# Block-sparse attention feeding a gMLP: one matmul at a time in the attention's slots, and a changed ending

## The chip, the cores and the metric

One core of a Trainium2 chip runs the whole program. The metric is the device time of one execution in microseconds; the times before are 11 executions with a median of 226.93 us, from 226.41 to 228.16. The engines are named as in the profile: PE (matrix multiplication; its weight loads have a row of their own, PEld), DVE (vector), ACT (activation), POOL (general purpose) and SP (which here only issues transfers).

## The reference, cut to what matters

Four batches, eight heads, 768 positions, 64 channels a head. Attention is masked in blocks of 32 positions (neighbours, first and last block, three sampled blocks a row); its output, with heads side by side, is the input x of a gated MLP that also mixes positions.

```
scores = where(mask, q @ k.T / sqrt(64), -1e9)          # 768 x 768 per head
attn   = softmax(scores)
x      = attn @ v                                        # heads joined: (4, 768, 512)
h      = relu(x @ w_in)                                  # (4, 768, 1024)
u, v   = h[..., :512], h[..., 512:]
v_n    = (v - mean(v)) / sqrt(var(v) + 1e-6)
v_s    = w_spatial @ v_n + b_spatial[:, None]            # mixes the 768 positions
out    = (u * v_s) @ w_out                               # (4, 768, 512)
```

## The kernel before, in words

Operands are bf16, sums are kept in PSUM in fp32. The 32 heads are worked in 16 pairs (`p` 0 to 15, four pairs to a batch). The order of instructions on every engine is the order in which the Python loop writes them down (a manual schedule): no planner moves anything. Each engine works off its own list in order, and a pool of tiles with a tag and a number of buffers (`bufs`) makes an instruction wait until the tile that had the buffer last is done with.

The loop at L461 goes through *slots*, twelve to a pair, six to a head. In a slot:

- `qk_exp` (L284) makes 128 rows of scores for one head: two matmuls of 384 columns into a PSUM tile of tag "sc" (two buffers), and one exp of 768 columns on ACT, which empties it into `a_all`.
- then come pieces of preparation of later pairs in fixed slots: `split_pair` (L275, slots 5 and 9) copies transposed k and q of the next pair on DVE, two copies each; `prepare` (L116, slot 7) casts k, q and v of pair p+2 to bf16 on POOL (`nat_k`, `nat_q`, `vv`); `tr_dma` (slot 10) has SP transpose them.
- then gMLP work of the batch before, if there is any (below).
- `av` (L298), seven slots behind `qk_exp`: six matmuls of 65 columns for one block of 128 queries, into tag "av". After the sixth block of a head, `norm` (L312) divides by the softmax sums on DVE. After each pair, x is transposed (`xtr`, L334): by SP for three pairs of a batch, by PE and a copy on DVE for the fourth.

The gMLP of a batch is 24 *units* (`moe_units`, L360), four groups of six: v (L376) and u (L399) are four matmuls of 512 columns each, s (the spatial product, L421) six, o (L437) four: 108 matmuls. Each unit has a PSUM tile of tag "moe" (two buffers, shared with transposes) and is followed by what empties it: v by relu on DVE (`vsb`), and by statistics of the row (`stats`, `mv`), every third v also by `std` and `rstd` on POOL; u by relu on ACT (`un`), and by the normalised `vn` on DVE; s by the gate on DVE (`gn`) and a transpose by SP (`gt`); o by a copy (`osb`, ACT for even ones and DVE for odd ones) and its transfer to `out` by SP. Below, v0 to v5, u0 to u5, s0 to s5 and o0 to o5 are these units.

The units of a batch become available in slot 8 of the pair after its last, and are handed to the next 48 slots: each slot adds its share of nanoseconds to a budget, and a whole unit is written down where the budget covers half of it:

```
budget += sum(u[0] for u in moe_q) / slots_left
slots_left -= 1
while moe_q and budget >= moe_q[0][0] / 2:
    ns, run = moe_q.popleft()
    run()
    budget -= ns
```

There are only 46 slots left for the third batch; what is not handed out by then comes after the loop (L525), one unit ahead of the last transpose of x, the rest behind it. The fourth batch then runs alone: its units take their PSUM tiles in turn from the tags "moe", "av" and "sc" (`moe_ps`, L352), v's relu is on ACT, and `gn` is transposed by PE (`g_tr`, L412).

Of the kernel before, what the change touches and what calls it, by code (L numbers as in the profile page):

```python
# [11 lines left out]
BF16 = mybir.dt.bfloat16  # L12
I32 = mybir.dt.int32
AF = mybir.ActivationFunctionType
# [12 lines left out]
def kernel(  # L27
# [16 lines left out]
    nc = tc.nc  # L44

    B, H, S, D = q.shape
# [3 lines left out]
    NCH = S // 128  # L50
    HALF = S // 2
    DM = H * D
    DFF = moe_w_in.shape[1]
    DH = DFF // 2
    NDM = DM // 128
    NDH = DH // 128
    NG = H // 2
    NP = B * NG
# [6 lines left out]
    psum = ctx.enter_context(tc.tile_pool(name="psum", bufs=1, space=bass.MemoryType.PSUM))  # L65
# [4 lines left out]
    w_in_t = const.tile([128, NDM, DFF], BF16)  # L70
    w_out_t = const.tile([128, NDH, DM], BF16)
    ws_nat = const.tile([128, NCH, S], BF16)
    w_spt = const.tile([128, NCH, S], BF16)
# [134 lines left out]
    for r in range(NR):  # L208
# [9 lines left out]
                         func=AF.Copy)  # L218
# [13 lines left out]
    tr_ps = {}  # L232
# [89 lines left out]
    def xtr_third(p, third):  # L322
        if third == 0:
            xt_ref[p] = work.tile([128, S], BF16, tag="xt", bufs=8, name="xt")
            tr_ps["x"] = psum.tile([128, S], BF16, tag="moe", bufs=2, name="ps_x")
        ps = tr_ps["x"]
        for c in (2 * third, 2 * third + 1):
            nc.tensor.transpose(out=ps[:, c * 128:(c + 1) * 128], in_=xn_ref[p][:, c],
                                identity=ident)
        if third == 2:  # L330
            xn_ref.pop(p)
            nc.vector.tensor_copy(out=xt_ref[p], in_=ps)
# [14 lines left out]
        nc.sync.dma_start_transpose(out=w_spt[:, :, tcc * 128:(tcc + 1) * 128],  # L347
                                    in_=ws_nat[:, tcc, :])

    tail_tags = deque(["sc", "av", "moe"])  # L350

    def moe_ps(last):  # L352
        if not last:
            return psum.tile([128, 512], FP32, tag="moe", bufs=2, name="ps_moe")
        tail_tags.rotate(1)
        if tail_tags[0] == "sc":
            return psum.tile([128, 1024], FP32, tag="sc", bufs=2, name="ps_sc")[:, 0:512]
        return psum.tile([128, 512], FP32, tag=tail_tags[0], bufs=2, name="ps_t")

    def moe_units(b):  # L360
        last = b == B - 1
        units = []
        un = work.tile([128, NCH, DH], BF16, tag="un", bufs=2)
        vsb = work.tile([128, NCH, DH], BF16, tag="vsb", bufs=2)
        vn = work.tile([128, NCH, DH], BF16, tag="vn", bufs=2)
        gn = work.tile([128, NCH, DH], BF16, tag="gn", bufs=2)
        gt = work.tile([128, NCH, NDH, 128], BF16, tag="gt", bufs=2)
        mv = work.tile([128, NCH, 2], FP32, tag="mv", bufs=2)
        std = work.tile([128, NCH], FP32, tag="std", bufs=2)
        rstd = work.tile([128, NCH], FP32, tag="rstd", bufs=2)  # L370

        def xt(g):
            return xt_ref[b * NG + g]

        for tcc in range(NCH):
            def v_unit(tcc=tcc):  # L376
                ps = moe_ps(last)
                for g in range(NDM):
                    nc.tensor.matmul(out=ps, lhsT=xt(g)[:, tcc * 128:(tcc + 1) * 128],  # L379
                                     rhs=w_in_t[:, g, DH:DFF],  # L380
                                     start=(g == 0), stop=(g == NDM - 1))
                if last:
                    nc.scalar.activation(out=vsb[:, tcc, :], in_=ps, func=AF.Relu)  # L383
                else:
                    nc.vector.tensor_scalar(out=vsb[:, tcc, :], in0=ps, scalar1=0.0,  # L385
                                            scalar2=None, op0=ALU.max)
                stats = work.tile([128, 6], FP32, tag="stats", bufs=2)
                nc.vector.bn_stats(out=stats, in_=vsb[:, tcc, :])  # L388
                nc.vector.bn_aggr(out=mv[:, tcc, :], in_=stats)  # L389
                if tcc % 3 == 2:  # L390
                    cs = slice(tcc - 2, tcc + 1)
                    nc.gpsimd.tensor_scalar(out=std[:, cs], in0=mv[:, cs, 1], scalar1=1e-6,  # L392
                                            scalar2=None, op0=ALU.add)
                    nc.gpsimd.tensor_tensor(out=rstd[:, cs], in0=std[:, cs],
                                            in1=mhalf[:, cs], op=ALU.pow)
            units.append((4 * 215, v_unit))

        for tcc in range(NCH):
            def u_unit(tcc=tcc):  # L399
                ps = moe_ps(last)  # L400
                for g in range(NDM):
                    nc.tensor.matmul(out=ps, lhsT=xt(g)[:, tcc * 128:(tcc + 1) * 128],  # L402
                                     rhs=w_in_t[:, g, 0:DH],
                                     start=(g == 0), stop=(g == NDM - 1))
                nc.scalar.activation(out=un[:, tcc, :], in_=ps, func=AF.Relu)
                nc.vector.tensor_scalar(out=vn[:, tcc, :], in0=vsb[:, tcc, :],
                                        scalar1=mv[:, tcc, 0:1],
                                        scalar2=rstd[:, tcc:tcc + 1],
                                        op0=ALU.subtract, op1=ALU.mult)
            units.append((4 * 215, u_unit))  # L410

        def g_tr(tcc):  # L412
            ps = psum.tile([128, S], BF16, tag="moe", bufs=2, name="ps_g")
            for dhc in range(NDH):
                nc.tensor.transpose(out=ps[:, dhc * 128:(dhc + 1) * 128],
                                    in_=gn[:, tcc, dhc * 128:(dhc + 1) * 128],
                                    identity=ident)
            act_copy(gt[:, tcc].rearrange("p c n -> p (c n)"), ps[:, 0:DH])

        for tcc in range(NCH):  # L420
            def s_unit(tcc=tcc):  # L421
                ps = moe_ps(last)
                for sc in range(NCH):
                    nc.tensor.matmul(out=ps, lhsT=w_spt[:, sc, tcc * 128:(tcc + 1) * 128],  # L424
                                     rhs=vn[:, sc, :],
                                     start=(sc == 0), stop=(sc == NCH - 1))
                nc.vector.scalar_tensor_tensor(out=gn[:, tcc, :], in0=ps,  # L427
                                               scalar=b_col[:, tcc:tcc + 1],
                                               in1=un[:, tcc, :], op0=ALU.add, op1=ALU.mult)
                if not last:  # L430
                    nc.sync.dma_start_transpose(out=gt[:, tcc], in_=gn[:, tcc, :])
                elif tcc > 0:
                    g_tr(tcc - 1)
            units.append((6 * 215, s_unit))

        for tcc in range(NCH):
            def o_unit(tcc=tcc):  # L437
                if last and tcc == 1:
                    g_tr(NCH - 1)
                ps = moe_ps(last)  # L440
                for dhc in range(NDH):
                    nc.tensor.matmul(out=ps, lhsT=gt[:, tcc, dhc, :],  # L442
                                     rhs=w_out_t[:, dhc, :],
                                     start=(dhc == 0), stop=(dhc == NDH - 1))
                osb = work.tile([128, DM], FP32, tag="osb", bufs=6)
                if tcc % 2 == 0:
                    nc.scalar.activation(out=osb, in_=ps, func=AF.Copy)
                else:
                    nc.vector.tensor_copy(out=osb, in_=ps)  # L449
                nc.sync.dma_start(  # L450
                    out=out[b].rearrange("(p c) d -> c p d", c=NCH)[tcc], in_=osb)
            units.append((4 * 215, o_unit))
        return units


    moe_q = deque()
# [4 lines left out]
    for p in range(NP + 1):  # L461
        for s in range(12):
# [38 lines left out]
                if p in (0, 1, 4, 6):  # L501
                    cast_weights((2, 2, 0, 0, 3, 0, 2)[p])
            if moe_q and slots_left > 0:
                budget += sum(u[0] for u in moe_q) / slots_left
                slots_left -= 1
                while moe_q and budget >= moe_q[0][0] / 2:
                    ns, run = moe_q.popleft()
                    run()
                    budget -= ns
            if g >= LAG:  # L510
                ja, qc = divmod(g - LAG, NCH)
                av(ja, qc)
# [6 lines left out]
            if s == 8 and p >= NG:  # L519
                xtr(p - 1)  # L520
                if p % NG == 0:
                    moe_q.extend(moe_units(p // NG - 1))
                    slots_left = 48
                    budget = 0.0
    if moe_q:  # L525
        moe_q.popleft()[1]()
    xtr(NP - 1)
    moe_q.extend(moe_units(B - 1))
    while moe_q:
        moe_q.popleft()[1]()  # L530

# [1 line left out]
_INS = ['q', 'k', 'v', 'sampled_blocks', 'moe_w_in', 'moe_w_spatial', 'moe_b_spatial', 'moe_w_out']  # L533
_OUTS = [((4, 768, 512), 'float32')]
# [25 lines left out]
```

The softmax here doesn't subtract the row's maximum and nothing guards it: scores larger than these inputs give would overflow.

## Time and profile before

| what | value |
|---|---|
| median of 11 runs | 226.93 us (226.41 to 228.16) |
| the profiled execution | 226.58 us, of which the span of its instructions is 224.8 us |
| PE busy | 213.6 us, 95% of the span |
| ACT busy | 171.2 us, 76% |
| DVE busy | 132.2 us, 59% |
| POOL busy | 64.2 us, 29% |
| clock granted to PE | 1.000 throughout |
| pairs 0 to 3, attention alone | up to about 48.8 us |
| batches 0, 1, 2 of the gMLP in the slots | 48.8 to 98.8, 98.8 to 148.9, 148.9 to 195.5 us |
| batch 3 of the gMLP alone | 196.2 to 221.8 us, then the last transfer |

The page of a profile gives busy time by engine, the span in 40 slices, the chain of work that ended last, and groups of instructions with the mean duration of one and what the engine waited for before them. A timeline gives start, duration, engine, line, operation, output and inputs, and how many instructions were merged into the row; a bracket at the end is idle time before the row and who ended it. A matmul's end is modelled, and the next one starts before it: 378 ns are shown for a matmul of 512 columns, but in a row of them one starts every 215 to 216 ns. So PE's real gaps are read from starts: a matmul of 512 columns is taken as 0.2155 us, one of 384 columns as 0.162, one of 65 columns as 0.0325.

### The profile page before, as it was taken

To read this page: it belongs to the slowest core of one execution; us is meant where nothing else is said; L and a number is where in the kernel's file an instruction comes from. 1 tells how busy PE (TensorE), PEld (TensorE's weight loads), DVE (VectorE), ACT (ScalarE), POOL (GpSimd) and SP (SyncE) were. 2 spreads that over 40 slices of the span, in tenths; PEclk is the share of its full clock that TensorE was granted. 3 is DMA by queue.
4 is the path that set the end of the run, shared out by engine and by line. 5 is a ranking of instruction groups with operands and counts; after the bars stand their busy time and mean duration, and the time that the engine had idled before them with its cause. 6 is when DMAs were issued, how large, how long until landed. Compare 5 with 4: busy or idle time off the path is not lost.

```text
span 224.8 us, 5286 instructions
## 1 busy us (share of the span) xinstructions
PE 213.6 (95%) x2119; PEld 130.3 (58%) x2148; DVE 132.2 (59%) x282; ACT 171.2 (76%) x245; POOL 64.2 (29%) x88
## 2 busy tenths in 40 slices
PE   7889999999999999999999999999999999999993
PEld 3557777766656555666556555666565555544551
DVE  6676446359994434379993434469983323674532
ACT  5799999998798677877898668877898666266351
POOL 5336761259483301211273001211230000012000
PEclk9999999999999999999999999999999999999999
DMA  6679989947997994999365665999050424610016
GB/s 178 243 230 389 388 295 394 379 64 97 269 235 145 276 107 135 227 356 297 124 114 204 119 85 169 213 304 242 0 105 3 82 50 83 231 52 0 0 50 235
DMA packets 56093, 40.27 MB, mean 179 GB/s; under 512 B 39300, under 2 KB 51588, under 8 KB 56068
## 3 DMA queue, kind: packets, MB, share of 16 engines
q1 hardware_dynamic: 55780, 39.53, 65.0%
q10 hardware_dynamic: 288, 0.39, 0.6%
q8 instruction: 17, 0.28, 0.5%
q14 instruction: 8, 0.07, 0.1%
HBM read 24.38 MB, written 6.29 MB: 136 GB/s over the span
## 4 chain that ended last, share of the span: by engine, by line
PE 73%; ACT 16%; DMA 5%; issue 2%; SPq 1%; POOL 1%; DVE 1%; POOLq 0%
PE ps L289 20%; ACT a_all L293 16%; PE ps_av L305 11%; PE ps_moe L424 10%; PE ps_moe L379 7%; PE ps_moe L442 7%; PE ps_moe L402 7%; DMA st_k<-in_k_dram 5%; PE ps_t L424 2%; PE ps_t L379 2%; PE ps_t L442 2%; PE ps_t L402 1%; PE ps_sc L424 1%; PE ps_sc L402 1%; PE ps_sc L442 1%
## 5 line engine op out<-in xcount | busy, mean ns | idle before, releaser
L293 ACT ACTIVATE a_all<-ps 128x768 bf16<-128x768 f32 x192 | 143.1, 812 | 30.1 <-PE ps L289 29.9
L289 PE MATMUL ps<-qt,kt 88*128 88x384 bf16 x384 | 93.5, 324 | 4.1 <-ACT a_all L293 2.8
L305 PEld LDWEIGHTS <-a_all 128*128 128x128 bf16 x1152 | 60.3, 98 | 28.5
L305 PE MATMUL ps_av<-vv,a_all 128*128 128x65 bf16 x1152 | 67.6, 194 | 0.0
L289 PEld LDWEIGHTS <-kt 88*128 88x128 bf16 x384 | 28.9, 97 | 8.1 <-issue 5.2
L427 DVE SCALAR_TENSOR_TENSOR gn<-ps_moe,b_col,un 128x512 bf16<-128x512 f32 x18 | 13.5, 751 | 27.2 <-PE ps_moe L424 27.2
L112 POOL CAST vv<-st_v 128x768 bf16<-128x768 f32 x16 | 13.6, 849 | 50.1 <-PE ps_av L305 45.9
L424 PE MATMUL ps_moe<-vn,w_spt 128*128 128x512 bf16 x99 | 24.8, 378 | 0.5
L424 PEld LDWEIGHTS <-w_spt 128*128 128x128 bf16 x144 | 13.8, 97 | 14.3
L392 POOL TENSOR_SCALAR std<-mv 128x3 f32<-128x3 f32 x8 | 1.9, 242 | 65.2 <-DVE mv L389 53.9
L109 POOL CAST nat_k<-st_k 128x768 bf16<-128x768 f32 x15 | 12.5, 833 | 22.0 <-DMA st_k<-in_k_dram 14.6
L319 DVE TENSOR_TENSOR xn<-ps_av,rc 128x384 bf16<-128x384 f32 x32 | 17.8, 557 | 1.1
L442 PE MATMUL ps_moe<-w_out_t,gt 128*128 128x512 bf16 x66 | 18.2, 378 | 0.3
L379 PE MATMUL ps_moe<-w_in_t,xt 128*128 128x512 bf16 x66 | 18.0, 378 | 0.3
L402 PE MATMUL ps_moe<-w_in_t,xt 128*128 128x512 bf16 x66 | 17.7, 378 | 0.3
L388 DVE BATCH_NORM_STATS2 stats<-vsb 128x6 f32<-128x512 bf16 x24 | 16.7, 694 | 1.9 <-ACT vsb L383 1.3
L379 PEld LDWEIGHTS <-xt 128*128 128x128 bf16 x96 | 9.3, 97 | 10.0 <-issue 0.7
L449 DVE COPY osb<-ps_moe 128x512 f32<-128x512 f32 x9 | 6.2, 692 | 15.0 <-PE ps_moe L442 14.9
L402 PEld LDWEIGHTS <-xt 128*128 128x128 bf16 x96 | 9.3, 97 | 9.5
L442 PEld LDWEIGHTS <-gt 128*128 128x128 bf16 x96 | 8.9, 97 | 8.4
L318 DVE RECIPROCAL rc<-ps_av 128x6 f32<-128x6 f32 x32 | 6.0, 187 | 13.1 <-PE ps_av L305 12.9
L385 DVE TENSOR_SCALAR vsb<-ps_moe 128x512 bf16<-128x512 f32 x18 | 12.3, 682 | 1.5 <-PE ps_moe L379 1.4
(82 smaller groups left out, 200.0 us busy)
## 6 DMA issues: line engine op xcount, KB each, us to landing
st_v<-in_v_dram SPq DMA_DIRECT2D x16, 384.0 KB, 5.3
out_dram<-osb SPq DMA_DIRECT2D x24, 256.0 KB, 2.7
st_q<-in_q_dram SPq DMA_DIRECT2D x15, 384.0 KB, 4.4
st_k<-in_k_dram SPq DMA_DIRECT2D x15, 384.0 KB, 5.5
wst<-in_moe_w_spatial_dram SPq DMA_DIRECT2D x3, 768.0 KB, 7.2
wst<-in_moe_w_in_dram SPq DMA_DIRECT2D x4, 512.0 KB, 8.9
wst<-in_moe_w_out_dram SPq DMA_DIRECT2D x2, 512.0 KB, 6.9
st_k<-in_k_dram ACTq DMA_DIRECT2D x2, 192.0 KB, 2.8
```

Of the source, the lines that this page charges most:

```text
L109: eng.tensor_copy(out=dst, in_=src)
L112: nc.gpsimd.tensor_copy(out=vv[p % 3][:, :, :, 0:D], in_=st.pop(("v", p)).rearrange("p h (c d) -> p h c d", d=D))
L289: nc.tensor.matmul(out=ps[:, hf * 512:hf * 512 + HALF], lhsT=kt[j % 4][:, ci * 128:(ci + 1) * 128], rhs=qt[j % 4][:, hf * HALF:(hf + 1) * ...
L293: nc.scalar.activation(out=a_ref[j][:, ci, :].rearrange("p (b c) -> p b c", b=2), in_=ps.rearrange("p (b c) -> p b c", b=2)[:, :, 0:HALF], ...
L305: nc.tensor.matmul(out=av_ref[j][:, qc, :], lhsT=a_ref[j][:, ci, qc * 128:(qc + 1) * 128], rhs=vv[p % 3][:, h, ci, :], start=(ci == 0), st ...
L319: nc.vector.tensor_tensor(out=xn_ref[p][:, :, h, :], in0=ps[:, :, 0:D], in1=rc.to_broadcast([128, NCH, D]), op=ALU.mult)
L379: nc.tensor.matmul(out=ps, lhsT=xt(g)[:, tcc * 128:(tcc + 1) * 128], rhs=w_in_t[:, g, DH:DFF], start=(g == 0), stop=(g == NDM - 1))
L388: nc.vector.bn_stats(out=stats, in_=vsb[:, tcc, :])
L402: nc.tensor.matmul(out=ps, lhsT=xt(g)[:, tcc * 128:(tcc + 1) * 128], rhs=w_in_t[:, g, 0:DH], start=(g == 0), stop=(g == NDM - 1))
L424: nc.tensor.matmul(out=ps, lhsT=w_spt[:, sc, tcc * 128:(tcc + 1) * 128], rhs=vn[:, sc, :], start=(sc == 0), stop=(sc == NCH - 1))
L427: nc.vector.scalar_tensor_tensor(out=gn[:, tcc, :], in0=ps, scalar=b_col[:, tcc:tcc + 1], in1=un[:, tcc, :], op0=ALU.add, op1=ALU.mult)
L442: nc.tensor.matmul(out=ps, lhsT=gt[:, tcc, dhc, :], rhs=w_out_t[:, dhc, :], start=(dhc == 0), stop=(dhc == NDH - 1))
```

## The change

The list of units becomes a list of single matmuls. A helper `add` writes a unit as n steps: the first step takes the PSUM tile, the last one is followed by what empties it (the old tail of the unit, now a function `..._post`). A slot's budget is counted in matmuls: 108 over 48 slots, two or three to a slot. For the third batch the matmuls are spread as if there were 52 slots, and half of what is left after the loop goes ahead of the last transpose of x, the other half behind it. The last transpose of x takes its PSUM tile from "sc" in place of "moe"; the turn of the tags in the fourth batch is sc, moe, av in place of moe, av, sc; and the very last copy is written as two halves, one on ACT and one on DVE.

```diff
@@ xtr_third
-            tr_ps["x"] = psum.tile([128, S], BF16, tag="moe", bufs=2, name="ps_x")
+            tr_ps["x"] = psum.tile([128, S], BF16, tag="moe" if p < NP - 1 else "sc", bufs=2,
+                                   name="ps_x")
@@ moe_ps
-    tail_tags = deque(["sc", "av", "moe"])
+    tail_tags = deque(["av", "sc", "moe"])
...
-        tail_tags.rotate(1)
+        tail_tags.rotate(-1)
@@ moe_units
+        def add(n, operands, post):
+            box = []
+
+            def step(i):
+                if i == 0:
+                    box.append(moe_ps(last))
+                lhs, rhs = operands(i)
+                nc.tensor.matmul(out=box[0], lhsT=lhs, rhs=rhs,
+                                 start=(i == 0), stop=(i == n - 1))
+                if i == n - 1:
+                    post(box[0])
+            units.extend((lambda i=i: step(i)) for i in range(n))
+
         for tcc in range(NCH):
-            def v_unit(tcc=tcc):
-                ps = moe_ps(last)
-                for g in range(NDM):
-                    nc.tensor.matmul(out=ps, lhsT=xt(g)[:, tcc * 128:(tcc + 1) * 128],
-                                     rhs=w_in_t[:, g, DH:DFF],
-                                     start=(g == 0), stop=(g == NDM - 1))
+            def v_post(ps, tcc=tcc):
...
-            units.append((4 * 215, v_unit))
+            add(NDM, lambda g, tcc=tcc: (xt(g)[:, tcc * 128:(tcc + 1) * 128],
+                                         w_in_t[:, g, DH:DFF]), v_post)
...
@@ o units
-                if tcc % 2 == 0:
+                if last and tcc == NCH - 1:
+                    nc.scalar.activation(out=osb[:, 0:DM // 2], in_=ps[:, 0:DM // 2],
+                                         func=AF.Copy)
+                    nc.vector.tensor_copy(out=osb[:, DM // 2:DM], in_=ps[:, DM // 2:DM])
+                elif tcc % 2 == 0:
...
@@ the loop
-                budget += sum(u[0] for u in moe_q) / slots_left
+                budget += len(moe_q) / slots_left
                 slots_left -= 1
-                while moe_q and budget >= moe_q[0][0] / 2:
-                    ns, run = moe_q.popleft()
-                    run()
-                    budget -= ns
+                while moe_q and budget >= 0.5:
+                    moe_q.popleft()()
+                    budget -= 1
...
-                    slots_left = 48
+                    slots_left = 48 if p < NP - NG else 52
...
-    if moe_q:
-        moe_q.popleft()[1]()
+    for _ in range(len(moe_q) // 2):
+        moe_q.popleft()()
     xtr(NP - 1)
     moe_q.extend(moe_units(B - 1))
     while moe_q:
-        moe_q.popleft()[1]()
+        moe_q.popleft()()
```

More of the change, by code (lines that the diff above doesn't have):

```diff
@@ L395, in v_unit, with u_post @@
                                             in1=mhalf[:, cs], op=ALU.pow)
-            units.append((4 * 215, v_unit))
+            add(NDM, lambda g, tcc=tcc: (xt(g)[:, tcc * 128:(tcc + 1) * 128],
+                                         w_in_t[:, g, DH:DFF]), v_post)
         for tcc in range(NCH):
[L399 to L404, printed above, removed]
+            def u_post(ps, tcc=tcc):
                 nc.scalar.activation(out=un[:, tcc, :], in_=ps, func=AF.Relu)
@@ L409, in u_unit @@
                                         op0=ALU.subtract, op1=ALU.mult)
-            units.append((4 * 215, u_unit))
+            add(NDM, lambda g, tcc=tcc: (xt(g)[:, tcc * 128:(tcc + 1) * 128],
+                                         w_in_t[:, g, 0:DH]), u_post)
         def g_tr(tcc):
@@ L420, in moe_units, with s_post @@
         for tcc in range(NCH):
[L421 to L426, printed above, removed]
+            def s_post(ps, tcc=tcc):
                 nc.vector.scalar_tensor_tensor(out=gn[:, tcc, :], in0=ps,
@@ L433, in s_unit, with o_post @@
                     g_tr(tcc - 1)
-            units.append((6 * 215, s_unit))
+            add(NCH, lambda sc, tcc=tcc: (w_spt[:, sc, tcc * 128:(tcc + 1) * 128],
+                                          vn[:, sc, :]), s_post)
         for tcc in range(NCH):
[L437 to L444, printed above, removed]
-                osb = work.tile([128, DM], FP32, tag="osb", bufs=6)
-                if tcc % 2 == 0:
+            def o_post(ps, tcc=tcc):
+                osb = work.tile([128, DM], FP32, tag="osb", bufs=6)
+                if last and tcc == NCH - 1:
[3 more added lines that the diff above has]
+                elif tcc % 2 == 0:
                     nc.scalar.activation(out=osb, in_=ps, func=AF.Copy)
@@ L451, in o_unit @@
                     out=out[b].rearrange("(p c) d -> c p d", c=NCH)[tcc], in_=osb)
-            units.append((4 * 215, o_unit))
+            if last and tcc == 1:
+                units.append(lambda: g_tr(NCH - 1))
+            add(NDH, lambda dhc, tcc=tcc: (gt[:, tcc, dhc, :], w_out_t[:, dhc, :]), o_post)
         return units
```

## The prediction

> **What bounds the kernel now.** I read the chain of work that ended last first, then PE's groups, then timelines of single stages.
>
> ```profile
> PE 73%; ACT 16%; DMA 5%; issue 2%; SPq 1%; POOL 1%; DVE 1%; POOLq 0%
> ...
> L293 ACT ACTIVATE a_all<-ps 128x768 bf16<-128x768 f32 x192 | 143.1, 812 | 30.1 <-PE ps L289 29.9
> L289 PE MATMUL ps<-qt,kt 88*128 88x384 bf16 x384 | 93.5, 324 | 4.1 <-ACT a_all L293 2.8
> ```
>
> PE is on the chain for 73%, ACT's exp for 16%. Most of that 16% is pairs 0 to 3, where a slot's PE work is below one exp and no gMLP exists yet; the change touches nothing there. From 48.8 us PE paces. A slot is 2x0.162 + 6x0.0325 = 0.52 us on PE, and each gMLP matmul adds 0.2155; the exps start 0.705 us apart when back to back. What is left to gain is the 2.8 us (14 times) in which PE waited for exps. They lie in the s stage, whose units are six matmuls handed to every second or third slot:
>
> ```profile
> 172.93 0.35 PE L305 MATMUL ps_av<-vv,a_all 128*128 128x65 bf16 x6
> 173.12 0.49 PE L289 MATMUL ps<-qt,kt 88*128 88x384 bf16 x2
> 173.45 0.36 PE L305 MATMUL ps_av<-vv,a_all 128*128 128x65 bf16 x6
> 173.99 0.48 PE L289 MATMUL ps<-qt,kt 88*128 88x384 bf16 x2 [0.18 <-ACT a_all L293]
> 174.31 1.46 PE L424 MATMUL ps_moe<-vn,w_spt 128*128 128x512 bf16 x6
> ...
> 173.13 2.21 ACT L293 ACTIVATE a_all<-ps 128x768 bf16<-128x768 f32 x3 [0.76 <-PE ps L289]
> ```
>
> Two slots in a row hold no unit; PE writes scores faster than exp empties the two "sc" buffers, and the third slot waits. By starts the gap is 173.99 - (173.45 + 0.195) = 0.345 us. It stands four times in each of batches 0, 1 and 2: 12 x 0.345 = 4.14 us. Elsewhere in the slots PE starts matmuls without a gap, except 0.09 us at the opening of batches 1 and 2.
>
> **The change part by part.** *Handing out single matmuls* puts two or three into every slot: 0.95 or 1.17 us against an exp of 0.705, so no run of empty slots is left and the 4.14 us go. In the u stage ACT needs 0.705 + 0.505 (`un`) x 2.25/4 = 0.99 us a slot against PE's 1.00, so PE stays just ahead. More changes between shapes cost nothing: after 384, 512 and 65 columns the next start comes after 0.162, 0.2155 and 0.0325 whatever follows.
>
> *What it adds.* A unit's PSUM tile is now open for about 1.8 us and the next unit opens at once, so the tile must be emptied within one unit; before, 0.5 to 1 us of other work lay between. Who empties late? DVE in the v stage:
>
> ```profile
> 107.56 0.69 DVE L278 COPY kt<-tt_k 64x768 bf16<-64x768 bf16 x2
> 108.17 0.68 DVE L385 TENSOR_SCALAR vsb<-ps_moe 128x512 bf16<-128x512 f32 x1
> ...
> 109.71 0.66 DVE L385 TENSOR_SCALAR vsb<-ps_moe 128x512 bf16<-128x512 f32 x1
> ...
> 112.22 1.38 DVE L278 COPY qt<-tt_q 64x768 bf16<-64x768 bf16 x2
> ...
> 111.72 0.89 POOL L394 TENSOR_TENSOR rstd<-std,mhalf 128x3 f32<-128x3 f32 x1
> 112.56 0.82 POOL L109 CAST nat_k<-st_k 128x768 bf16<-128x768 f32 x1
> 113.33 0.95 POOL L109 CAST nat_q<-st_q 128x768 bf16<-128x768 f32 x1
> ```
>
> A v unit keeps DVE 1.55 to 1.6 us; a norm (0.67) and a pair of k copies (0.61) come between. The second `rstd` held POOL's casts back until 112.6. In the changed order v5 ends one slot later, after slot 7's `prepare`, so `nat_k`, `nat_q` and `vv` stand ahead of the second `rstd` and run during the k copies.
>
> Batch 1, step by step. Its clock starts at 98.90 (98.81 plus the 0.09, which stays: o5 still ends in the last slot, and v0 waits for its copy). The order of the changed program has 2,3,2,2,2,2,3,2,2,3,2 matmuls in its first slots. v1 ends with slot 4's first, ready for DVE 0.20 later at 102.71 (102.20 before); v1 1.55, norm 0.67: v2 starts at 104.93, its statistics end at 106.56. POOL: `std` and `rstd` take 1.29 more, so casts run from 107.8 to 108.6 and 109.4. DVE: v3 ends and the k copies start at 108.07, beside both casts. Without casts they take 0.61; with them, as two `vn` beside casts did (1.63 at 113.63), about 1.5. v4's emptying then starts at 109.57, takes 0.68, and releases PE 0.06 later (as 196.18 to 196.24 in the ending): 110.31. u0, which takes v4's buffer, is due with the 25th matmul: ten slots (10.16) + 0.325 + 0.2155 after 98.90, 109.60. **PE stalls 0.71.** v4's statistics, norm(9) and v5's emptying end at 112.53; u1 is due at 111.50 + 0.71: **0.32** more. Batch 0 (clock 48.83): POOL's weight casts hold `rstd` until 58.2 as before; the k copies start at 58.0, so the first is free and the second meets `nat_k` (together 1.25); v4's buffer is released at 59.94 for a u0 due at 59.53, **0.41**, and v5's at 62.16 for a u1 due at 61.43 + 0.41, **0.32**. Batch 2 hands out 2.08 matmuls a slot, so the 25th comes in slot 12: u0 is due 11.22 after its clock and released at 11.39, **0.17**; u1 13.12 + 0.17 and 13.61, **0.32**. Sum of the three: 2.25 us.
>
> Bounds: if no cast meets the copies, 0.14 in batches 0 and 1 remain, 0.3; if every k copy takes the 1.00 us that the slower of the two q copies at 112.22 took, pairs of 2.0 make it 4.0. The Trainium skill ("SBUF — State Buffer", section "Who interferes with whom") says that such a copy and a POOL instruction exclude each other for whole instructions. In batch 1 the second copy would then wait out `nat_q` and still need its 0.34, some 0.4 us later than by the row; with that in each batch the sum is about 3.3. I take the row: 2.25.
>
> *Moved without a price.* The second `rstd` behind three casts: `vv` waits for slot 6's `av`, is through by 110.2, and v5's statistics end only at 113.4. `vn`3 runs after norm(10), from about 117; s0 opens near 121. On SP, `gt`5 goes behind two transposes of k and q (about 1.2 us each on its queue) in batches 0 and 1, and x of a pair behind a `gt` or the reverse; `gt` lands in 2.5 us, o5 comes 20 matmuls and 9 slots, 9 us, after s5. Loads are issued one output copy earlier.
>
> *The ending.*
>
> ```profile
> 194.43 1.02 PE L442 MATMUL ps_moe<-w_out_t,gt 128*128 128x512 bf16 x4
> 195.48 0.51 PE L328 MATMUL ps_x<-ident,xn 128*128 128x128 bf16 x6
> 196.24 1.89 PE L379 MATMUL ps_t<-w_in_t,xt 128*128 128x512 bf16 x8 [0.25 <-DVE osb L449]
> ...
> 221.09 0.69 DVE L449 COPY osb<-ps_sc 128x512 f32<-128x512 f32 x1 [1.04 <-PE ps_sc L442]
> ```
>
> Two gaps by starts: 0.18 ahead of the transposes (the norm) and 0.42 behind them (v0's "moe" buffer, waiting for o5's copy). Twelve matmuls are now left: six (1.29) cover the norm, which took 1.05 from `av` to transpose; six cover the copy of x; x and v0 are on "sc", free since the last exp. 0.60 us go. The other tags have the same two buffers each at the same distance: nothing.
>
> *The last copy.* Side by side, halves would end 0.27 earlier. But the Trainium skill ("PSUM — Partial Sum Buffer", section "PSUM bank collisions raise a hardware error") forbids ACT and DVE one bank at once, reads too; no run here shows it. The order of the changed program agrees: the DVE half waits for ACT's 245th and last instruction, the ACT half. ACT half: 0.60 less the step from 768 to 512 columns (0.81 - 0.60), 0.39, bounded by 0.30 and 0.60; DVE half: 0.69 less twice the 0.135 from 384 (0.557) to 512, 0.42, bounded by 0.35 and 0.69; handoff 0.03 (vsb to stats), ACT 0.04 later to start: 0.88 against 0.69. It costs 0.19 (0.03 to 0.67).
>
> Sum: -4.14 - 0.60 + 2.25 + 0.19 = -2.30. The profiled execution took 226.58 (span 224.8), 0.35 below the median; on the median 226.93 - 2.30 = **224.6 us**, the span about 222.5.
>
> **The rivals.**
>
> *The casts miss the copies* (22%). They meet only if POOL is on `nat_k` at DVE's k copies, 0.3 us after it starts in my walk. Then 0.3 in place of 2.25: 222.7.
>
> *The stalls are twice as large* (13%): a stall pushes the next emptying later, or v2 and v3 wait as well, where I find 0.7 and 0.9 us of room: 226.9, about no change.
>
> *Slower: ACT empties the u units too late* (7%). Place: u2 to s1, six openings a batch, each needing the `un` of two units before. Room: a unit lasts 1.79; 0.24 to start, up to one exp (0.705) and 0.60 make 1.55. With a second exp ahead of `un` it is 2.25 and PE waits 0.46; 0.3 on average, 18 times, is 5.4: 230.0. It turns the forecast into a loss from 0.13 each. For it speaks 0.99 against 1.00 above; against it, `un` is written in the slot of its last matmul, behind one exp alone, and a wait of PE lets ACT catch up.
>
> *The change doesn't remove the gaps* (5%): if they had another cause than empty slots, only the ending gains: 226.93 - 0.60 + 2.44 = 228.8. All 12 follow two slots without a unit.
>
> **How the numbers follow.** My forecast has 53%, its own range 223.6 to 225.7 (its stalls at 1.3 to 3.3). 0.2% (0.45 us) is about what a measurement here can tell. Faster: 53 + 22 + 5 of the 13 = 80%; within: 3; slower: 5 of the 13 + 7 + 5 = 17. The range 222.3 to 227.0 leaves out the two slow rivals and the outer ends of the others.
>
> **What would show it.** Right: no wait of L289 for exps from 48.8 us on; in each of batches 0 to 2 a PE gap at u0 (0.2 to 0.7) and at u1 (0.3) released by DVE's `vsb`; two k copies of 1.3 us or more together beside `nat_k`; no gap at x's last transpose; the halves of the last copy one after the other. Wrong: k copies of 0.6 (then 222.7), or PE waiting for `un` (then slower).

## The result and the profile after

The changed kernel takes 225.03 us (median of 12 runs, 224.11 to 226.08) against 226.93 us (226.4 to 228.29) of the kernel before: a ratio of 0.991, 95% interval 0.989 to 0.993. By the ratio it is 2.1 us faster (1.7 to 2.5; the medians lie 1.9 apart); forecast were 2.3. Three single runs further down, two of the four with the new handing alone and one of the twenty with the ending alone, took 273 to 364 us at a granted clock of 0.56 to 0.76 and are left out of the ratios.

The profiled execution took 226.08 us, with a span of 224.2, so span against span it gains only 0.6 us on the one before. The rest is hidden by its start: up to the transpose of x of pair 3, where the gMLP begins and which the change doesn't reach, it took 50.06 us against 48.49. So the two are compared from that point. The table has the lengths, read from the starts of PE's transposes of x (the last but one column ends with the last instruction that writes `osb`):

| us | start to x of pair 3 | batch 0 | batch 1 | batch 2, to the last transpose of x | from there to the last `osb` | sum without the start |
|---|---|---|---|---|---|---|
| before | 48.49 | 49.99 | 50.09 | 46.92 | 26.30 | 173.29 |
| after | 50.06 | 49.19 | 49.79 | 44.87 | 27.33 | 171.19 |

The difference of the sums is 2.10 us. (Batch 2 and the ending have to be read together, since the last transpose now comes earlier in the order: 72.20 against 73.22.)

The page of the changed kernel, the chain of work that ended last and the groups of instructions:

```profile
PE 69%; DVE 14%; ACT 13%; issue 2%; DMA 2%; SPq 0%
...
L293 ACT ACTIVATE a_all<-ps 128x768 bf16<-128x768 f32 x192 | 150.0, 817 | 21.6 <-PE ps L289 13.7
L289 PE MATMUL ps<-qt,kt 88*128 88x384 bf16 x384 | 94.6, 327 | 1.3 <-DVE qt L244 0.5
...
L385 PE MATMUL ps_moe<-w_in_t,xt 128*128 128x512 bf16 x130 | 39.6, 378 | 2.5 <-DVE vsb L396 1.7
```

DVE had 1% of the chain and now has 14%. Ahead of the scores (L289) PE stood idle for 4.1 us before, and now for 1.3, of which the exp is no longer the largest part. In its place the products with `w_in_t` (v and u) wait 1.7 us for `vsb`, the relu that empties a v unit on DVE. The list of PE's waits says the same; its columns are the time in total, how often, and the longest. After:

```profile
PE ps_moe L385 <- DVE vsb L396: 1.7, 4, 0.6
...
PE ps_moe L385 <- DVE gn L430: 0.3, 1, 0.3
PE ps L289 <- ACT a_all L293: 0.3, 1, 0.3
```

Before:

```profile
PE ps L289 <- ACT a_all L293: 2.8, 14, 0.3
```

The one wait for an exp that is left lies at 45.29 us, before the gMLP begins. The wait for `gn` was not forecast.

A timeline of PE in the s stage of batch 2, the place that the prediction showed with empty slots:

```profile
172.70 0.60 PE L385 MATMUL ps_moe<-vn,w_spt 128*128 128x512 bf16 x2
173.13 0.35 PE L305 MATMUL ps_av<-vv,a_all 128*128 128x65 bf16 x6
173.33 0.49 PE L289 MATMUL ps<-qt,kt 88*128 88x384 bf16 x2
173.65 0.59 PE L385 MATMUL ps_moe<-vn,w_spt 128*128 128x512 bf16 x2
```

Each of these slots holds two matmuls of the spatial product, and each row begins where the one before lets it (173.13 + 0.195 = 173.33). None of the twelve gaps of 0.345 us is left.

And PE in batch 1 where v passes into u, the place of the new stalls:

```profile
109.84 0.49 PE L289 MATMUL ps<-qt,kt 88*128 88x384 bf16 x2
110.17 0.38 PE L385 MATMUL ps_moe<-w_in_t,xt 128*128 128x512 bf16 x1
111.18 0.38 PE L385 MATMUL ps_moe<-w_in_t,xt 128*128 128x512 bf16 x1 [0.64 <-DVE vsb L396]
```

110.17 + 0.2155 is 110.38; u0 starts at 111.18, so PE stood for 0.80 us. DVE and POOL at that time:

```profile
108.78 1.75 DVE L278 COPY kt<-tt_k 64x768 bf16<-64x768 bf16 x2
110.46 0.68 DVE L396 TENSOR_SCALAR vsb<-ps_moe 128x512 bf16<-128x512 f32 x1
...
107.75 0.88 POOL L405 TENSOR_TENSOR rstd<-std,mhalf 128x3 f32<-128x3 f32 x1
108.60 0.82 POOL L109 CAST nat_k<-st_k 128x768 bf16<-128x768 f32 x1
109.37 0.95 POOL L109 CAST nat_q<-st_q 128x768 bf16<-128x768 f32 x1
```

The two copies of k start at 108.78 and last 1.75 us; POOL's casts run beside them all this time; then `vsb` empties v4, and 0.04 us after its end PE gets the buffer. Read by starts, the stalls are 0.27, 0.80 and 0.28 us at u0 and 0.31 each at u1 in batches 0, 1 and 2: 2.28 us in all.

### The profile page after: what moved, and what is told of

It reads as the page before. It is cut to its first block, busy times and chain, and to the rows that moved or that the text cites. A ratio compares the mean times of both kernels' runs of the same rounds, so it can differ in the third digit from the quotient of the medians.

```text
span 224.2 us, 5285 instructions
## 1 busy us (share of the span) xinstructions
PE 214.1 (96%) x2117; PEld 130.6 (58%) x2148; DVE 128.3 (57%) x282; ACT 177.6 (79%) x246; POOL 64.5 (29%) x88
## 4 chain that ended last, share of the span: by engine, by line
PE 69%; DVE 14%; ACT 13%; issue 2%; DMA 2%; SPq 0%
PE ps_moe L385 24%; PE ps L289 19%; ACT a_all L293 12%; PE ps_av L305 10%; PE ps_t L385 7%; DVE vsb L396 4%; DVE stats L399 4%; PE ps_sc L385 4%; PE wps L180 2%; DVE kt L278 2%; DMA st_q<-in_q_dram 2%; DVE xn L319 2%; PE ps L228 1%; DVE mv L400 1%; PE ps_g L423 1%
## 5 line engine op out<-in xcount | busy, mean ns | idle before, releaser
L293 ACT ACTIVATE a_all<-ps 128x768 bf16<-128x768 f32 x192 | 150.0, 817 | 21.6 <-PE ps L289 13.7
L289 PE MATMUL ps<-qt,kt 88*128 88x384 bf16 x384 | 94.6, 327 | 1.3 <-DVE qt L244 0.5
L385 PE MATMUL ps_moe<-w_in_t,xt 128*128 128x512 bf16 x130 | 39.6, 378 | 2.5 <-DVE vsb L396 1.7
L289 PEld LDWEIGHTS <-kt 88*128 88x128 bf16 x384 | 28.3, 98 | 4.0 <-issue 1.2
L385 PE MATMUL ps_moe<-vn,w_spt 128*128 128x512 bf16 x99 | 30.0, 378 | 0.5
L385 PE MATMUL ps_moe<-w_out_t,gt 128*128 128x512 bf16 x66 | 19.1, 378 | 0.5 <-DVE gn L430 0.3
L109 POOL CAST nat_q<-st_q 128x768 bf16<-128x768 f32 x15 | 12.9, 861 | 0.0
L278 DVE COPY kt<-tt_k 64x768 bf16<-64x768 bf16 x20 | 9.5, 476 | 3.6 <-DMA tt_k<-nat_k 3.5
L412 ACT ACTIVATE un<-ps_moe 128x512 bf16<-128x512 f32 x18 | 10.9, 608 | 0.0
```

What stands on the lines that cost most here:

```text
L109: eng.tensor_copy(out=dst, in_=src)
L278: nc.vector.tensor_copy(out=(qt if nm == "q" else kt)[(2 * p + h) % 4][0:D, :], in_=src[h * D:(h + 1) * D, :])
L289: nc.tensor.matmul(out=ps[:, hf * 512:hf * 512 + HALF], lhsT=kt[j % 4][:, ci * 128:(ci + 1) * 128], rhs=qt[j % 4][:, hf * HALF:(hf + 1) * ...
L293: nc.scalar.activation(out=a_ref[j][:, ci, :].rearrange("p (b c) -> p b c", b=2), in_=ps.rearrange("p (b c) -> p b c", b=2)[:, :, 0:HALF], ...
L385: nc.tensor.matmul(out=box[0], lhsT=lhs, rhs=rhs, start=(i == 0), stop=(i == n - 1))
```

## The experiments

Each kernel was compared in the table's way, since the run-to-run spread of a median is as large as some of the effects.

### The new handing alone, and the ending alone

The first kernel has the changed handing with the old tags and the old last copy; at most four leftover matmuls come ahead of the last transpose of x, and 48 slots are counted in the third batch.

From the changed kernel:

```diff
-    tail_tags = deque(["av", "sc", "moe"])
+    tail_tags = deque(["sc", "av", "moe"])
...
-                    slots_left = 48 if p < NP - NG else 52
+                    slots_left = 48
...
-    for _ in range(len(moe_q) // 2):
+    for _ in range(min(4, len(moe_q))):
```

(and `ps_x` on "moe", the turn by `rotate(1)`, and one copy at the end as before).

> Only the handing out of single matmuls (48 slots for every batch; four matmuls ahead of the last transpose of x, old tags, old last copy). My theory: 4.14 us of gaps at the scores of the s stage are gone, about 0.3 to 0.8 at u0 and 0.3 at u1 come in every batch (batch 2 as batch 1, since it has the same rate), the ending keeps its 0.60: 226.93 - 4.14 + 2.8 = about 225.6. Rival, that the added waits belong to the ending or to the 52 slots: 222.8.

Measured: ratio 0.993 (0.991 to 0.995), 225.4 us on the median before. The sum without the start is 172.10, that is 1.19 below before. The gaps by starts: none at the scores; u0 0.27, 0.80 and **0.79**, u1 0.31 each: 2.80 us. In batch 2 u0's stall is as large as in batch 1, while the changed kernel has only 0.28 there. That is what the count of 48 instead of 52 slots does: u0 comes due 0.5 us earlier, while the emptying doesn't (u0 starts 11.17 us after v0 in both kernels). At the last transpose of x it keeps 0.20 us ahead and has 0.60 behind. -4.14 + 2.80 + 0.20 (the ending's 0.80 against 0.60 before) = -1.14.

The second kernel has whole units, as before, with the changed ending except the split copy.

From the kernel before:

```diff
-            tr_ps["x"] = psum.tile([128, S], BF16, tag="moe", bufs=2, name="ps_x")
+            tr_ps["x"] = psum.tile([128, S], BF16, tag="moe" if p < NP - 1 else "sc", bufs=2,
+                                   name="ps_x")
...
-    tail_tags = deque(["sc", "av", "moe"])
+    tail_tags = deque(["av", "sc", "moe"])
...
-        tail_tags.rotate(1)
+        tail_tags.rotate(-1)
...
-                    slots_left = 48
+                    slots_left = 48 if p < NP - NG else 52
...
-    if moe_q:
+    for _ in range(len(moe_q) // 2):
```

> Whole units, but the turn of the tags, the tag of the last x and the 52 slots as changed, and the old last copy. Three units are left over, one goes ahead of the transpose and two behind it. My theory: the 0.42 us gap behind the transpose goes, the 0.18 ahead of it stays, all twelve gaps at the scores stay: 226.5. Rival, that the spacing of 52 slots moves the waits of the third batch: a change of 0.5 us or more there either way.

Measured: ratio 0.9986 (0.9965 to 1.0008); the sum is 172.89, 0.40 below before. All twelve gaps of 0.345 are there. The gap of 0.42 behind the transposes is gone, the 0.18 ahead of them is not:

```profile
192.83 0.81 PE L443 MATMUL ps_moe<-w_out_t,gt 128*128 128x512 bf16 x3
193.66 0.51 PE L329 MATMUL ps_x<-ident,xn 128*128 128x128 bf16 x6
194.00 1.89 PE L443 MATMUL ps_moe<-w_out_t,gt 128*128 128x512 bf16 x8
195.73 1.03 PE L380 MATMUL ps_sc<-w_in_t,xt 128*128 128x512 bf16 x4
```

(The first row holds the last three of the four matmuls ahead.) 192.83 + 3 x 0.2155 = 193.48 and the transposes start at 193.66: four matmuls ahead don't cover the norm. Behind them 194.00 + 8 x 0.2155 = 195.73: no gap. So the two halves of the ending's gain are worth 0.42 and 0.18, and the second needs more than four matmuls ahead, as the six in the changed kernel are.

### The last copy whole

From the changed kernel:

```diff
-                if last and tcc == NCH - 1:
-                    nc.scalar.activation(out=osb[:, 0:DM // 2], in_=ps[:, 0:DM // 2],
-                                         func=AF.Copy)
-                    nc.vector.tensor_copy(out=osb[:, DM // 2:DM], in_=ps[:, DM // 2:DM])
-                elif tcc % 2 == 0:
+                if tcc % 2 == 0:
```

> The changed kernel with the last copy whole on DVE. If the two halves stand one after the other, the end comes 0.15 to 0.2 us earlier: the last copy ends 0.89 us after its product by starts in place of 1.05, some 224.85. If they overlap in effect: 0.2 later than the changed kernel.

Measured: 224.62 us, ratio 0.990 (0.986 to 0.993), which can't tell 0.2 us from nothing; the trace can. The ending of the changed kernel:

```profile
218.48 1.89 PE L385 MATMUL ps_t<-w_out_t,gt 128*128 128x512 bf16 x8
...
220.41 0.38 ACT L444 ACTIVATE osb<-ps_t 128x256 f32<-128x256 f32 x1 [0.22 <-PE ps_t L385]
220.82 0.43 DVE L446 COPY osb<-ps_t 128x256 f32<-128x256 f32 x1 [1.45 <-ACT osb L444]
```

and with one copy:

```profile
217.38 1.89 PE L385 MATMUL ps_t<-w_out_t,gt 128*128 128x512 bf16 x8
...
219.30 0.69 DVE L446 COPY osb<-ps_t 128x512 f32<-128x512 f32 x1 [1.03 <-PE ps_t L385]
```

The last product is through at 218.48 + 8 x 0.2155 = 220.20 and at 219.10; the output is written 1.05 and 0.89 us later. DVE's half names ACT's half as what it waited for: the two run one after the other, and the split costs 0.16 us.

### The casts behind the second rstd

If POOL's casts make the k copies slow, u0 and u1 must come on time once the casts stand behind the second `rstd` again. In this kernel, pairs 5, 9 and 13 (the second pair of each gMLP batch) write slot 7's `prepare` down after the slot's gMLP matmuls. From the changed kernel, first at its old place, then behind the matmuls:

```diff
-                prepare(p + 2)
+                late = p >= NG and p % NG == 1
+                if not late:
+                    prepare(p + 2)
...
+            if s == 7 and NG <= p < NP - 2 and p % NG == 1:
+                prepare(p + 2)
```

> The changed kernel, with the casts of k, q and v in slot 7 of the second pair of every batch written after the slot's gMLP matmuls, so that the second rstd stands ahead of them on POOL. If casts beside the k copies make v4's buffer late: the k copies take 0.6 us together, the gaps at u0 (0.27, 0.80, 0.28) go, those at u1 (0.31 each) shrink to 0.15 or less, about 223.2. Rival, that the buffer held over two slots is too short for DVE whatever POOL does: the gaps stay, 225.0.

Measured: 223.78 us, ratio 0.984 (0.981 to 0.988), which is 223.4 on the median before. Batch 0 goes from 49.19 to 48.67, batch 1 from 49.79 to 48.74. Batch 2 stays at 44.87, and it is the control: there v5 ends in slot 8, one slot too late for this edit, so the casts still stand ahead of the second `rstd`. DVE's and POOL's timelines in batch 1, then in batch 2:

```profile
108.26 0.69 DVE L278 COPY kt<-tt_k 64x768 bf16<-64x768 bf16 x2
108.87 0.68 DVE L396 TENSOR_SCALAR vsb<-ps_moe 128x512 bf16<-128x512 f32 x1
...
113.12 1.02 POOL L405 TENSOR_TENSOR rstd<-std,mhalf 128x3 f32<-128x3 f32 x1
114.03 0.82 POOL L109 CAST nat_k<-st_k 128x768 bf16<-128x768 f32 x1
...
157.06 1.68 DVE L278 COPY kt<-tt_k 64x768 bf16<-64x768 bf16 x2
...
156.81 0.82 POOL L109 CAST nat_k<-st_k 128x768 bf16<-128x768 f32 x1
157.58 0.95 POOL L109 CAST nat_q<-st_q 128x768 bf16<-128x768 f32 x1
```

In one execution the same two copies take 0.69 us with POOL idle and 1.68 with `nat_k` and `nat_q` beside them. PE in batch 1 and in batch 2:

```profile
109.64 0.59 PE L385 MATMUL ps_moe<-w_in_t,xt 128*128 128x512 bf16 x2
...
158.90 0.87 PE L385 MATMUL ps_moe<-w_in_t,xt 128*128 128x512 bf16 x2
```

A row of two such matmuls shows 0.59 to 0.60 us when nothing is between them. The 0.87 in batch 2 holds u0's stall of 0.28 inside a merged row. In batches 0 and 1 u0 comes without a gap and u1 with 0.05. So the stalls follow the k copies' collision with the casts: with the same handing and the same two PSUM buffers, PE waits 0.05 us at most without it. (Whether the collision is enough by itself is seen in the last experiment.)

### The o units of pair 16 on the scores' buffers

The gap that wasn't forecast stands in batch 2 behind the last exp. PE and DVE of the changed kernel:

```profile
189.50 0.35 PE L305 MATMUL ps_av<-vv,a_all 128*128 128x65 bf16 x6
190.15 0.38 PE L385 MATMUL ps_moe<-w_out_t,gt 128*128 128x512 bf16 x1 [0.29 <-DVE gn L430]
...
188.65 0.20 DVE L318 RECIPROCAL rc<-ps_av 128x6 f32<-128x6 f32 x1 [1.16 <-PE ps_av L305]
188.88 0.56 DVE L319 TENSOR_TENSOR xn<-ps_av,rc 128x384 bf16<-128x384 f32 x1
189.35 0.74 DVE L430 SCALAR_TENSOR_TENSOR gn<-ps_moe,b_col,un 128x512 bf16<-128x512 f32 x1
```

In pair 16 no scores are left to compute, and a slot lasts 0.62 us instead of 0.95. The norm of the last but one head stands ahead of s5's gate `gn` on DVE, `gn` ends at 190.09, and o1, which takes s5's buffer, waits for it. The gap is 0.45 by starts; a PE record is missing in it (o0's last matmul, 0.2155), which leaves 0.24. In the kernel with one copy, where the record is there, the same gap is 0.24. In the next kernel the o units begun in pair 16 take the two "sc" buffers, which are free by then. From the changed kernel:

```diff
-                    box.append(moe_ps(last))
+                    box.append(psum.tile([128, 1024], FP32, tag="sc", bufs=2,
+                                         name="ps_o")[:, 0:512]
+                               if in_16[0] and not last else moe_ps(last))
...
+            in_16[0] = p == NP
```

> The changed kernel, with the output units of the third batch that open in pair 16's slots on PSUM tag sc, which no scores need any more. The 0.24 us gap at the first matmul of o1 stands where slots have no scores and last only 0.6 us, so that s5's buffer is wanted back 1.2 us after its end, while DVE does norm(30) before the gate. If so, the gap goes and nothing else moves: 0.24 us less, about 224.8. If DVE itself were what PE lacks there, a gap of the same size comes at another o unit.

Measured: 225.12 us, ratio 0.991 (0.988 to 0.994): the times can't tell 0.24 us. In the trace batch 2 goes from 44.87 to 44.64 and the rest stays (49.20, 49.79, 27.32). DVE is as late as it was (`gn` starts 0.70 us after the norm's `rc`, as in the changed kernel), but no product of o waits for it any more.

### All three mended, and only the s units in single steps

The first kernel puts together one last copy, o on "sc" in pair 16, and the casts behind the matmuls of slot 8 in place of slot 7, so that batch 2 is reached too (the line below against the edit above).

```diff
-            if s == 7 and NG <= p < NP - 2 and p % NG == 1:
+            if s == 8 and NG <= p < NP - 2 and p % NG == 1:
                 prepare(p + 2)
```

> The changed kernel with the last copy whole, pair 16's output units on sc, and the casts of the second pair of every batch at the end of slot 8 in place of slot 7, so that they stand behind the second rstd in the third batch too (there v5 ends in slot 8). My theory: no gap above 0.1 at u0 or u1 in any batch, none at o1: 225.0 - 2.1 - 0.24 - 0.17 = about 222.5. Rival, that DVE's own load keeps u1 waiting: 0.3 a batch stay, 223.3.

Measured: 223.18 us, ratio 0.983 (0.979 to 0.987). Its batches take 48.66, 48.87 and 44.06, the ending 27.17. u0 and u1 come on time in all three (0.05 at most). A new gap of 0.13 stands in batch 1 at an o product (144.72).

The other way round is to leave v, u and o as whole units, as before, and take apart only s, whose six matmuls in a row had made the empty slots. From the kernel before:

```diff
+            def s_step(sc, tcc=tcc, box=box):
+                if sc == 0:
+                    box.append(moe_ps(last))
...
-            units.append((6 * 215, s_unit))
+            units.extend((215, lambda sc=sc, step=s_step: step(sc)) for sc in range(NCH))
```

> The kernel before, with only the spatial units handed out one matmul at a time; v, u and o stay whole, budget in ns, the ending as before. If all of the gain lies in the s stage and all of the loss in v and u, the twelve gaps go and no gap comes at u0 or u1: 226.93 - 4.14 = 222.8. If whole v and u units beside single s matmuls still leave runs of empty slots in which PE waits for exps, less: 224 to 225.

Measured: 223.67 us, ratio 0.984 (0.980 to 0.987), 223.2 on the median before. The sum without the start is 169.17, 4.12 below before, where the twelve gaps were 4.14. PE has no gap at the scores, nor at u0 and u1; only the two of 0.09 at the opening of a batch and the ending's 0.18 and 0.42 are left. PE between u0, which began at 108.80, and u1 (the last row) in batch 1:

```profile
109.85 0.49 PE L289 MATMUL ps<-qt,kt 88*128 88x384 bf16 x2
110.18 0.36 PE L305 MATMUL ps_av<-vv,a_all 128*128 128x65 bf16 x6
110.37 0.49 PE L289 MATMUL ps<-qt,kt 88*128 88x384 bf16 x2
110.70 1.03 PE L402 MATMUL ps_moe<-w_in_t,xt 128*128 128x512 bf16 x4
```

As in the kernel before, the casts miss the k copies here (the two copies take 0.69 us), so this kernel alone doesn't say whether the stalls are gone for want of a collision or because a slot without gMLP work, in which nothing asks for a buffer, leaves DVE time to empty one. It does say that the gain of the new handing was in taking the s units apart, and the loss at u0 and u1 in taking v and u apart.

The last kernel adds the changed tags, 52 slots and two leftover units ahead of the last transpose of x to it, with the last copy whole. From the kernel with only s in single steps, besides the tags:

```diff
-                    slots_left = 48
+                    slots_left = 48 if p < NP - NG else 52
...
-    if moe_q:
+    for _ in range((len(moe_q) + 1) // 2):
```

> The same with the ending as changed (turn of the tags, last x on sc, 52 slots for the third batch, two of the left units ahead of the last transpose), last copy whole on DVE. 222.8 less the 0.60 us of the two gaps around the transpose: 222.2. If the leftovers bring a wait of their own, 222.5 or more.

Measured: **223.02 us**, ratio 0.982 (0.979 to 0.985); the sum is 168.62. Batch 2 and ending together take 71.29 against 71.85 with only s in single steps, 0.56 less where the two gaps were 0.60. The timeline of PE round the last transposes:

```profile
188.29 1.89 PE L448 MATMUL ps_moe<-w_out_t,gt 128*128 128x512 bf16 x8
190.01 0.50 PE L329 MATMUL ps_x<-ident,xn 128*128 128x128 bf16 x6
190.35 1.03 PE L448 MATMUL ps_moe<-w_out_t,gt 128*128 128x512 bf16 x4
191.21 1.03 PE L380 MATMUL ps_sc<-w_in_t,xt 128*128 128x512 bf16 x4
```

188.29 + 8 x 0.2155 = 190.01, and 190.35 + 4 x 0.2155 = 191.21: both gaps are gone. This is faster than the kernel before, and by 0.9% than the changed one. The kernel with all three mended can't be told from it by the times (their intervals overlap).

This kernel also parts the two causes. With 52 slots v5 comes later in batch 2, and there the casts do meet the k copies:

```profile
154.54 1.67 DVE L278 COPY kt<-tt_k 64x768 bf16<-64x768 bf16 x2
156.13 0.67 DVE L386 TENSOR_SCALAR vsb<-ps_moe 128x512 bf16<-128x512 f32 x1
...
157.64 1.03 PE L403 MATMUL ps_moe<-w_in_t,xt 128*128 128x512 bf16 x4
```

The copies take 1.67 us, as in the changed kernel (1.68), but v4's buffer is free at 156.81 and u0 asks for it only at 157.64. PE has no gap at u0 or u1. The kernel with the ending alone shows the same in its batch 2. So it takes both for a stall: the collision, and v and u units that follow one another without a slot between.

## Why the prediction was right

Its sum, term by term, against the traces:

| step | predicted | measured |
|---|---|---|
| twelve gaps at the scores in the s stage | -4.14 | -4.14, none is left |
| two gaps at the last transpose of x | -0.60 | -0.60, none is left |
| stalls at u0 (batches 0, 1, 2) | 0.41 + 0.71 + 0.17 | 0.27 + 0.80 + 0.28 |
| stalls at u1 | 3 x 0.32 | 3 x 0.31 |
| last copy in two halves | +0.19 | +0.16 |
| other tags, "nothing" | 0 | +0.24 at o1 |
| sum | -2.30 | -2.06; the table of stages says -2.10 |

*The gain.* That the empty slots make the gaps is shown twice: with only s in single steps they are gone and the sum drops by 4.12; with only the ending changed all twelve stay.

*The stalls.* The mechanism was right: `vsb` late by k copies that run beside `nat_k` and `nat_q`. The working counted from the start of the first copy to the start of the emptying behind them. By this count the pair took 1.14 us in batch 0 (predicted 1.25), 1.67 in batch 1 (1.5) and 1.60 in batch 2, and with POOL idle 0.61, as taken. Moving the casts took away 1.06 us of stalls in batch 1 and 0.53 in batch 0, and left batch 2, which the edit doesn't reach, as it was. The total of 2.28 against 2.25 is closer than its terms, and that is luck: u0 was 0.14 too high in batch 0 and 0.09 and 0.11 too low in batches 1 and 2. "1.3 or more" for all three pairs was said too roughly, since the working itself had 1.25 for batch 0.

*Row or rule.* By the row the sum of the stalls was 2.25, by the rule of the Trainium skill ("SBUF — State Buffer", "Who interferes with whom": the loser waits for whole instructions) about 3.3. The runs gave 2.28, so the row had the better price. They don't speak against the rule, though. In the trace of the changed kernel five copies of k run into a cast, and each ends 0.21 us after that cast, whenever it began: in batch 1 `nat_k` and `nat_q` end at 109.42 and 110.32, the copies at 109.63 and 110.53. Three q copies of the kernel before end 0.21 us after their casts too. So a copy does wait until the cast is over. What the working overcharged is the rest: it put a copy's whole 0.34 behind the cast, where 0.21 remained. Its "some 0.4 us later" doesn't come out of its own times either: 109.4 + 0.34 is 109.74, 0.17 behind the row's 109.57.

*The last copy.* The halves came one after the other, 0.38 and 0.43 (estimated 0.39 and 0.42). What two engines reading one bank at once would do, no run here shows.

*What failed* is "The other tags have the same two buffers each at the same distance: nothing", together with the room that the working took for the tiles of s and o. I had measured that room by a unit's length of 1.8 us in slots with scores. In pair 16 a slot is a third shorter, so a unit takes 1.2, and norm and gate together (1.44 us from 188.65 to 190.09) no longer fit. It cost 0.24, and the gap goes when the o units get other buffers.

*The rivals.* The casts did meet the copies; the stalls were not twice as large; the gaps were due to empty slots; and ACT did not empty u late: no wait of PE for `un` stands in the list of waits, so 0.99 us against 1.00 a slot was enough.

*The runs' expectations* came out up to 0.9 us too low as times: the kernel with all three mended, the one with only s in single steps and the one with the ending as well were expected at 222.5, 222.8 and 222.2 and ran at 223.18, 223.67 and 223.02. As stages they were right: 4.43, 4.13 and 4.73 us below before were expected, and the sums without the start are 4.52, 4.12 and 4.67 below. What differs lies outside these stages. A part is the start (below). Another lies outside the span: the profiled execution of the last kernel took 222.60 us with a span of 219.8, which leaves 2.8 us, where the kernel before leaves 1.8. The other runs have no trace, so what they lost, and where, stays open.

## What to carry to other kernels

Before work is handed out in finer pieces, find the stage in which the coarse pieces leave a gap, and take only that one apart: a pause between units on the busy engine can be the time in which another engine empties its buffers (0.83 us of room at u0 in the last kernel, where the changed one waits). An accumulator's room is a unit's period less what the emptying engine has queued ahead of it, and it must be reckoned again wherever the period shrinks, as at the end when one of two interleaved streams runs dry. And look at what the shift of an order puts beside each other on DVE and POOL: here one slot's delay of v5 brought the casts beside the copies and, with no pause left, took back 2.28 us of a gain of 4.74.

## What the runs showed of the hardware that was not expected

The start of an execution varies by up to 2 us with the same instructions. Up to the transpose of x of pair 3, which no kernel here changes, the profiled executions of the nine other kernels took 48.1 to 50.1 us and that of the kernel before 48.49. In the profile after, 1.46 of its 1.57 us are lost by 7.33 us. PE there, after:

```profile
4.70 0.85 PE L228 MATMUL ps<-ident,nat_k 128*64 128x128 bf16 x6
...
7.33 0.82 PE L180 MATMUL wps<-warm 128*128 128x128 bf16 x6
...
11.14 0.52 PE L228 MATMUL ps<-ident,nat_k 128*64 128x128 bf16 x6
```

and before:

```profile
4.32 0.52 PE L228 MATMUL ps<-ident,nat_k 128*64 128x128 bf16 x6
...
5.87 0.51 PE L180 MATMUL wps<-warm 128*128 128x128 bf16 x6
```

At 4.70 us the six transposes start one every 107 ns in the profile after, at 11.14 one every 56 ns, and in that before they do so from 4.32 on. In all ten profiled executions PE begins at the slow pace (the first matmuls on `warm`, of 512 columns, start 0.43 us apart in place of 0.2155) and goes over to the fast one at a moment that differs: at 3.87 us before, at 10.40 after, from 3.83 to 10.63 over the ten. The page's granted clock of 1.00 throughout doesn't show this. The record of the granted clock in the trace itself begins only at that moment, 3.87 and 10.40 us, and what lies ahead of it was counted as full speed. What decides the moment was not tried. Where the program is the same, the stages behind the start repeat to 0.02 us (batch 0 takes 49.19 or 49.20 in four kernels), which is why the small effects here are read from stages and not from times.

Also not expected was how little of a collision POOL bears: with the copies elsewhere `nat_k` takes 0.82 us and `nat_q` 0.88, beside them 0.82 and 0.95, while each of the copies goes from 0.35 to 0.84 (the kernel with the casts behind, batches 1 and 2).
